# Attention with one factor product, one mask and a two-part Y; weights decoded 768 columns at a time; a new order for the first 512 tokens

## The chip, the cores and the metric

The kernel runs on one core of one Trainium2 chip. The metric is the device time of one execution in microseconds (us), the median of three runs. On the core work TensorE (matrix products; PE in the views, PEld its weight loads), VectorE (DVE), ScalarE (ACT), GpSimd (POOL) and SyncE (SP), which here only issues DMA transfers. Each engine runs its instructions in the order in which they are written and waits for semaphores where it needs another's result.

## The reference

A linear attention with a decaying state, then two expert layers in a row, all of them on float32 inputs (the weights are float64, as they come out of a product with a float64 scalar):

```python
for t in range(S):                      # S = 768, 4 batches, 8 heads, D = 48
    cur = np.einsum('bhd,bhe->bhde', u[None] * kt, vt)
    y[:, :, t] = np.einsum('bhd,bhde->bhe', rt, state + cur)
    state = wt[:, :, :, None] * state + np.einsum('bhd,bhe->bhde', kt, vt)
...
h = x @ w_in                            # x: 3072 x 384, w_in: 384 x 2048
x = (h * np.clip(h + 3.0, 0.0, 6.0) / 6.0) @ w_out
...
a, b = x @ w_a, x @ w_b                 # 384 x 1536 each
out = a * b @ w_out2
```

## The kernel before

**Units.** The tokens are cut into 6 blocks of 128 per batch; a block of a batch is a unit, 24 in all, unit n being block n // 4 of batch n % 4. The attention of a unit works on two chunks of 64 tokens. Its factors lie with the head dimension on partitions: 48 rows of even heads from partition 0, 48 of odd heads from 64, and 4 head pairs side by side along the columns. One tile `rkw` of 1545 columns holds r (0 to 511), k (512 to 1023) and the decays w (from 1024).

**One unit, by its letters** (the order below is written in them; a number after a letter is the unit, slot or weight piece). R, N, V load r/k/w, the token-major copy (r, k, v) and v. z (L191) and s (L215) scan the decays backwards and forwards; c (L199, L200) takes the chunk products pc and their reciprocals as seeds of s. k (L206) multiplies k by z, a and b (L223) multiply r by pp for the even and the odd heads: a on VectorE, b on GpSimd, both into the tile `yo`. T transposes k on TensorE, t copies the result. A (L298, L299) is k against r within a chunk, on TensorE; m and M (L303) mask its two halves into `yo`. So `yo` holds, per head half, the scaled r (48 rows) and under or over it the masked A (64 rows), with zero rows between. K is k against v, in PSUM; u and f (L337) scale the state by pc for the two chunks, v and g (L344, L345) copy it beside the loaded v in the tile `vs`, and e and h (L355) add K to it. Y (L366) is then one product of 128 or 112 rows per head and chunk: scaled r with the state and masked A with v in one. d, D, o form r·u·k per head (for units 0 and 1 by TensorE, `PE_DOT`; for the others by GpSimd products and a reduction on VectorE, L259), O (L266) multiplies it by v, x (L380) adds it to Y. X transposes the result, H and L (L395, L400) split it into a high part and a rest, `xh` and `xl`.

**Expert layers.** They work in slots: 128 columns of the first layer's 2048 on 512 tokens. P (L497, nine products into one bank) is the first layer, r y G l its activation and its split (L518, L522, L526, L531), Q (L550, nine products) the second. A slot needs `xh` and `xl` of all four units of a block. 96 slots for both layers are followed by 72 steps of the third and fourth.

**Weights.** They come as float64 and are decoded by integer steps in half pieces of 384 columns, 32 for the first two layers and 36 later: W loads one into `raw` (3 buffers), i (L451, L452) scales its two words on ScalarE, j (L457) shifts and J (L461) sets the sign on VectorE, w (L467) adds on GpSimd, p (L482) takes the high part on ScalarE and n (L487) the low part on VectorE or GpSimd.

**Order.** `prepare` (L719) loads unit 0, sets constants and zeros in `vs`, and gives TensorE idle products. `start` (L864) then goes through the string `CFG["start"]`, letter by letter: units 0 to 7, slots 0 to 15 and half pieces 0 to 31. `CFG["pool"]` lists what goes to GpSimd there instead of VectorE. From slot 16 on `run` (L808) goes slot by slot: elementwise work of the attention stages that are due, P, then T and A of a unit in its stage 1, the activation, Q of the slot before, weight work, and the other stages' products. A unit passes stages 0 to 5 in six slots, a new unit starts every third slot, and units 8 to 23 go that way. SP issues loads in the same order: R for the unit after next in stage 1, V in stage 3, N in stage 4.

Of the kernel before, what the change touches and what calls it, by code (L numbers as in the profile page):

```python
# [964 lines left out]
```

## Time and profile before

| what | us |
|---|---|
| median of 3 runs | 1040.18 (1039.97 to 1040.42) |
| span of the profiled execution | 1038.7 |
| TensorE busy in the span | 989.7 (95%) |
| VectorE busy | 656.7 (63%) |
| ScalarE busy | 376.3 (36%) |
| GpSimd busy | 245.3 (24%) |

The profile is of one execution. It gives that execution's span from the first to the last instruction; a run's time also holds what lies around the span, and the median stands 1.5 us above this span. Shares are means over the whole span, which has a hand-ordered part and a regular one, so they are read together with the stretches and the chain of waits.

### The profile page before, as it was taken

Reading aid. Unit: us, or ns where it says so; the run is one execution under the profiler, and the core shown is the slowest. Engines: PE = TensorE matmul, PEld = TensorE weight load, DVE = VectorE, ACT = ScalarE, POOL = GpSimd, SP = SyncE. Lnnn points to the kernel's source line nnn. Section 1 sums busy time; section 2 is a strip of 40 time slices with the busy share of each in tenths; the row PEclk is TensorE's granted clock in tenths of the full one; section 3 lists DMA queues with packets and bytes.
Section 4 is the critical chain, followed back from the end, with each engine's and each line's share of the span. In section 5 each row is a group of like instructions: output and inputs, shape, how many; then the busy total and the mean of one; then the engine's idle time right before and its main releaser. Section 6 shows DMA issues by size and latency. Waiting matters only on the chain.

```text
span 1038.7 us, 15835 instructions
## 1 busy us (share of the span) xinstructions
PE 989.7 (95%) x6339; PEld 813.4 (78%) x6342; DVE 656.7 (63%) x1012; ACT 376.3 (36%) x727; POOL 245.3 (24%) x221
## 2 busy tenths in 40 slices
PE   7687889999999999999999999999999999999996
PEld 4465668778777877777777888888888888888886
DVE  8999996875775776776688886444444444422222
ACT  3356553233323333333667643222222222222121
POOL 5777772321230321132244531000000000000000
PEclk8698889999999999999999999999999999999999
DMA  9254463231222232120243531111111110100001
GB/s 323 94 175 152 138 205 123 70 116 56 99 70 84 72 114 91 62 70 1 92 132 123 180 119 32 51 42 31 51 42 32 58 53 22 41 21 13 19 1 34
DMA packets 33299, 85.79 MB, mean 83 GB/s; under 512 B 4160, under 2 KB 10816, under 8 KB 33216
## 3 DMA queue, kind: packets, MB, share of 16 engines
q1 hardware_dynamic: 33216, 84.69, 24.4%
q8 instruction: 52, 0.85, 0.3%
q14 instruction: 31, 0.25, 0.1%
HBM read 75.23 MB, written 9.44 MB: 82 GB/s over the span
## 4 chain that ended last, share of the span: by engine, by line
PE 65%; DVE 24%; issue 5%; ACT 4%; POOL 1%; DMA 0%; DVEq 0%; POOLq 0%
PE ab L497 29%; PE oa L618 15%; PE x2a L550 10%; PE h L497 9%; DVE t L522 3%; DVE wa L457 3%; DVE z L191 2%; ACT gh L526 2%; DVE gl L531 2%; DVE pp L215 2%; DVE yo L303 2%; DVE w L487 2%; DVE st L355 1%; DVE wa L461 1%; DVE sp L337 1%
## 5 line engine op out<-in xcount | busy, mean ns | idle before, releaser
L497 PE MATMUL ab<-xh_b,w 128*128 128x512 f32 x864 | 225.1, 396 | 0.0
L497 PEld LDWEIGHTS ab<-xh_b,w 128*128 128x128 f32 x864 | 161.2, 188 | 33.3 <-DVE t L522 0.4
L497 PE MATMUL h<-xh_a,w 128*128 128x512 f32 x576 | 164.8, 421 | 16.0 <-DVE w L487 9.3
L596 DVE TENSOR_TENSOR ta<-ab,ta 128x512 f32<-128x512 f32 x72 | 49.8, 691 | 198.3 <-PE ab L497 198.3
L550 PE MATMUL x2a<-gh,w 128*128 128x512 f32 x576 | 152.6, 400 | 1.4 <-ACT gh L526 1.2
L497 PEld LDWEIGHTS h<-xh_a,w 128*128 128x128 f32 x576 | 107.9, 196 | 43.1 <-DVE w L487 10.9
L550 PEld LDWEIGHTS x2a<-gh,w 128*128 128x128 f32 x576 | 106.1, 188 | 28.6 <-ACT gh L526 2.5
L497 PE MATMUL ab<-xl_b,w 128*128 128x512 f32 x432 | 124.1, 395 | 0.0
L531 DVE TENSOR_TENSOR gl<-t,gh 128x512 fp32r<-128x512 f32 x91 | 82.0, 901 | 60.3 <-ACT gh L526 55.0
L618 PE MATMUL oa<-w,ph 128*128 128x384 f32 x576 | 113.4, 338 | 0.0
L618 PEld LDWEIGHTS oa<-w,ph 128*128 128x128 f32 x576 | 102.9, 188 | 6.5 <-DVE x2e L562 0.2
L526 ACT CAST gh<-t 128x512 fp32r<-128x512 f32 x96 | 59.5, 620 | 130.2 <-DVE t L522 126.9
L599 ACT CAST ph<-ta 128x512 fp32r<-128x512 f32 x72 | 44.7, 621 | 165.9 <-DVE ta L596 165.9
L595 ACT COPY ta<-ab 128x512 f32<-128x512 f32 x72 | 42.2, 586 | 166.6 <-PE ab L497 166.6
L467 POOL TENSOR_TENSOR wa<-wa,raw 128x384 int32<-128x384 int32 x68 | 75.8, 1115 | 106.2 <-DVE wa L461 74.0
L522 DVE SCALAR_TENSOR_TENSOR t<-t,h 128x512 f32<-128x512 f32 x96 | 65.3, 681 | 52.4 <-ACT t L518 51.8
L497 PEld LDWEIGHTS ab<-xl_b,w 128*128 128x128 f32 x432 | 81.2, 188 | 19.8
L497 PE MATMUL h<-xl_a,w 128*128 128x512 f32 x288 | 85.4, 406 | 0.0
L518 ACT ACTIVATE t<-h,half 128x512 f32<-128x512 f32 x96 | 66.0, 687 | 46.8 <-PE h L497 43.5
L550 PE MATMUL x2a<-gl,w 128*128 128x512 f32 x288 | 82.9, 396 | 0.0
L600 DVE TENSOR_TENSOR pl<-ta,ph 128x512 fp32r<-128x512 f32 x72 | 49.9, 693 | 49.4 <-ACT ph L599 49.4
L223 POOL TENSOR_TENSOR yo<-rkw,pp 48x512 f32<-48x512 f32 (+1 forms) x25 | 37.3, 1493 | 160.1 <-DVE pp L215 83.8
(89 smaller groups left out, 1264.6 us busy)
## 6 DMA issues: line engine op xcount, KB each, us to landing
raw<-in_wall_dram SPq DMA_DIRECT2D x68, 384.0 KB, 3.1
rkw<-in_rkw_dram SPq DMA_DIRECT2D x23, 772.5 KB, 5.1
nat<-in_nat_dram SPq DMA_DIRECT2D x22, 576.0 KB, 3.9
cw<-in_rkw_dram SPq DMA_DIRECT2D x24, 260.5 KB, 2.7
vs<-in_vst_dram SPq DMA_DIRECT2D x48, 96.0 KB, 2.7
x2d<-x2e SPq DMA_DIRECT2D x18, 256.0 KB, 2.5
x2r<-x2d SPq DMA_DIRECT2D x18, 256.0 KB, 2.9
out_dram<-oe SPq DMA_DIRECT2D x24, 192.0 KB, 2.0
```

The source lines that it names most:

```text
L467: nc.gpsimd.tensor_tensor(out=a, in0=a, in1=raw[n][:, :, 0], op=ALU.add)
L497: nc.tensor.matmul(out=o, lhsT=lt, rhs=rt, start=(i == 0), stop=(i == 3 * n - 1))
L518: nc.scalar.activation(out=t, in_=hb[s], func=ACTF.Relu, bias=half, scale=1.0 / 6.0)
L522: nc.vector.scalar_tensor_tensor(out=t, in0=t, scalar=1.0, in1=hb.pop(s), op0=ALU.min, op1=ALU.mult)
L526: nc.scalar.copy(out=gh, in_=G["t", s])
L531: ve(f"l{s}").tensor_tensor(out=gl, in0=G.pop(("t", s)), in1=G[s][0].bitcast(F32), op=ALU.subtract)
L550: nc.tensor.matmul(out=acc1[i][k], lhsT=w[:, e, 384 + k * 128:512 + k * 128], rhs=rt, start=(f == 0 and e == 0 and rt is gh), stop=(f == N ...
L595: nc.scalar.copy(out=t, in_=a)
L596: nc.vector.tensor_tensor(out=t, in0=bb, in1=t, op=ALU.mult)
L599: nc.scalar.copy(out=gh, in_=t)
L600: nc.vector.tensor_tensor(out=gl, in0=t, in1=gh.bitcast(F32), op=ALU.subtract)
L618: nc.tensor.matmul(out=acc2[j][b][:, 0:384], lhsT=lt[:, b * 128:(b + 1) * 128], rhs=rt, start=(f == 0 and rt is wh and lt is ph), stop=(la ...
```

## The change

Five things are changed.

**One factor product.** The two scans now write into one tile `zp` of 1042 columns, the forward products in front and the backward ones behind, laid out so that r and k, which lie side by side in `rkw`, are multiplied by it in one instruction of 1024 columns on VectorE (k). a and b are gone. A reads both its operands from `rkw`.

**One mask.** A's halves come out in the order of the partitions, so m masks all 128 rows in one instruction, into a tile `am` of its own. M, `yo`, the zeroing of `vs` and the copies of the state into `vs` (v, g) are gone.

**Y from two products.** Per head and chunk, one product of the scaled r (48 rows) with the scaled state `sp` and one of the masked A (64 rows) with v, added in PSUM; even and odd heads go to two banks, and x adds them in two instructions. For units 0 to 3 the first chunk has no state and needs the second product alone. T and A of a unit now stand at the end of the slot with the other stages' products.

**Weights.** A piece has 768 columns and `raw` and `wa` two buffers each; J writes into `raw`, w is two additions on GpSimd or, for the seven pieces named in `CFG["fast"]`, one instruction of 1536 half words on VectorE, and n is always on VectorE.

**The order.** All units up to 7 form the dot by TensorE (`N_DOT = 8`), `CFG["pool"]` is empty, and the string is new. `prepare`, as before, begins with `load_rkw(0)`.

```diff
-    "fast": 'b6',
+    "pool": "",
+    "fast": "w4 w5 w6 w9 w11 w14 w15",
-        "z0 R1 c0 s0 a0 d0 D0 o0 b0 k0 z1 c1 A0 s1 W0 M0 i0 j0 W1 J0 m0 N0 d1 k1 i1 j1 a1 J1 R2 b1 O0 T0 t0 "
+        "R0 W0 V2 V1 V0 V3 R1 d0 N0 z0 D0 o0 c0 s0 W1 i0 k0 j0 A0 J0 T0 m0 w0 t0 z1 R2 N1 K0 c1 p0 d1 O0 s1 D1 e0 "
...
+    def a_s(n):
+        u = U[n]
+        nc.vector.tensor_tensor_scan(
+            out=u["zp"][:, 0:519], data0=u["rkw"][:, 1024:1543], data1=seed[:, 0:519], initial=0.0,
+            op0=ALU.mult, op1=ALU.add,
+        )
+
     def a_k(n):
         u = U[n]
+        rk = u["rkw"][:, 0:1024].rearrange("p (q i) -> p q i", i=64)
+        f = u["zp"][:, 0:1040].rearrange("p (q i) -> p q i", i=QL)[:, :, 0:64]
+        ve(f"k{n}").tensor_tensor(out=rk, in0=rk, in1=f, op=ALU.mult)
...
-                nc.tensor.matmul(out=a[64:128, sl], lhsT=kk[0:48, sl], rhs=Y[0:48, 0, sl], start=True, stop=True)
-                nc.tensor.matmul(out=a[0:64, sl], lhsT=kk[64:112, sl], rhs=Y[64:112, 1, sl], start=True, stop=True)
+                for e in (0, 64):
+                    nc.tensor.matmul(
+                        out=a[e:e + 64, sl], lhsT=kk[e:e + 48, sl], rhs=rr[e:e + 48, sl], start=True, stop=True,
+                    )
+    def a_m(n):
         u = U[n]
         nc.vector.tensor_tensor(
+            out=u["am"].rearrange("p (q i) -> p q i", i=64), in0=u["ap"].rearrange("p (q i) -> p q i", i=64),
+            in1=mask.rearrange("p (o i) -> p o i", o=1).to_broadcast([128, 8, 64]), op=ALU.mult,
         )
...
     def a_Y(n):
+        yp = u["yp"] = [att_bank(f"Y{e}", n) for e in range(2)]
         for p in range(NP):
+            for i in range(2):
                 for c in range(2):
                     sl = slice(p * 128 + c * 64, p * 128 + c * 64 + 64)
+                    first = j == 0 and c == 0
+                    if first and i == 0:
+                        continue
+                    for e in range(2):
+                        lo = 64 * e
+                        if i == 0:
+                            lt, rt = u["rkw"][lo:lo + 48, sl], u["sp", c][lo:lo + 48, p]
+                        else:
+                            lt, rt = u["am"][lo:lo + 64, sl], u["vs"][lo:lo + 64, p, c]
+                        nc.tensor.matmul(
+                            out=yp[e][64 * c:64 * c + 64, p * D:p * D + D], lhsT=lt, rhs=rt,
+                            start=i == 0 or first, stop=i == 1,
+                        )
...
+    def w_sign(i):
+        t = raw[i]
         nc.vector.scalar_tensor_tensor(
+            out=t[:, :, 0], in0=t[:, :, 1], scalar=-2 ** 31, in1=t[:, :, 0], op0=ALU.bitwise_and, op1=ALU.bitwise_or,
         )
+    def w_add(i, eng):
+        a, t = raw.pop(("a", i)), raw[i]
+        cuts = (0, 768) if eng is nc.vector else (0, 384, 768)
+        for c0, c1 in zip(cuts, cuts[1:]):
+            eng.tensor_tensor(out=a[:, c0:c1], in0=a[:, c0:c1], in1=t[:, c0:c1, 0], op=ALU.add)
...
-            for n, sg in act:
-                if sg == 1:
-                    att_pe(n, sg)
...
             for n, sg in act:
-                if sg != 1:
-                    att_pe(n, sg)
+                att_pe(n, sg)
```

What moves is shown at three places. The first is the beginning of SP's queue of loads (`rkw0` is unit 0's r, k and w, `raw` a weight piece, `vs` and `avs` hold v, `nat` the token-major copy). Before:

```order
L147 DMA rkw0_102<-in_rkw_dram 128x521
L148 DMA rkw0_102<-in_rkw_dram 128x1024
L727 DMA cst_sb_79<-in_cst_dram 128x194
L728 DMA u_pair_81<-in_ud_dram 128x8
L150 DMA rkw1_137<-in_rkw_dram 128x1545
L442 DMA raw0_179<-in_wall_dram 128x768
L442 DMA raw1_186<-in_wall_dram 128x768
```

Now:

```order
L136 DMA rkw0_99<-in_rkw_dram 128x521
L137 DMA rkw0_99<-in_rkw_dram 128x1024
L685 DMA cst_sb_79<-in_cst_dram 128x194
L686 DMA u_pair_81<-in_ud_dram 128x8
L136 DMA rkw0_124<-in_rkw_dram 128x521
L137 DMA rkw0_124<-in_rkw_dram 128x1024
L401 DMA raw0_127<-in_wall_dram 128x1536
L155 DMA avs2_95<-in_vst_dram 128x384
L155 DMA vs1_90<-in_vst_dram 128x384
L155 DMA vs0_89<-in_vst_dram 128x384
L155 DMA avs3_96<-in_vst_dram 128x384
L139 DMA rkw1_133<-in_rkw_dram 128x1545
```

Unit 0's two loads stand there twice, into two buffers, a weight piece of twice the width follows, and unit 1's load stands behind four loads of v.

The second is the end of the hand-written order on VectorE, before slot 16 (`w15` is the low part of the last weights, `gl` the rest of an activation, `xl_a1` the rest of a unit's output, `t` an activation). Before:

```order
L380 TENSOR_TENSOR nat7_1358<-Y_7_1557,nat7_1358 128x384
L522 SCALAR_TENSOR_TENSOR t13_1600<-t13_1600,h13_1539 128x512
L522 SCALAR_TENSOR_TENSOR t14_1603<-t14_1603,h14_1585 128x512
L400 TENSOR_TENSOR xl_a1_1137<-X_7_1596,xh_a1_1136 128x3x128
L457 TENSOR_SCALAR wa31_1620<-raw31_1487 128x384
L461 SCALAR_TENSOR_TENSOR wa31_1620<-raw31_1487,wa31_1620 128x384
L531 TENSOR_TENSOR gl12_1639<-t12_1524,gh12_1637 128x512
L531 TENSOR_TENSOR gl13_1652<-t13_1600,gh13_1650 128x512
L531 TENSOR_TENSOR gl14_1669<-t14_1603,gh14_1667 128x512
L522 SCALAR_TENSOR_TENSOR t15_1654<-t15_1654,h15_1608 128x512
L355 TENSOR_TENSOR st3_94<-K1_7_1498,sp7_1_1522 112x192
L531 TENSOR_TENSOR gl15_1697<-t15_1654,gh15_1695 128x512
```

Now:

```order
L360 TENSOR_TENSOR xl_a1_903<-X_6_1460,xh_a1_902 128x3x128
L446 TENSOR_TENSOR w15_1489<-wa15_1421,w15_1489 128x768
L309 TENSOR_TENSOR st3_94<-K0_7_1495,sp7_0_1423 112x192
L490 TENSOR_TENSOR gl14_1524<-t14_1468,gh14_1492 128x512
L298 TENSOR_TENSOR sp7_1_1526<-st3_94,pc7_1313 112x192
L309 TENSOR_TENSOR st3_94<-K1_7_1496,sp7_1_1526 112x192
L360 TENSOR_TENSOR xl_a1_903<-X_5_1253,xh_a1_902 128x3x128
L481 SCALAR_TENSOR_TENSOR t15_1567<-t15_1567,h15_1514 128x512
L337 TENSOR_TENSOR nat7_1181<-Y0_7_1530,nat7_1181 128x4x48
L337 TENSOR_TENSOR nat7_1181<-Y1_7_1531,nat7_1181 128x4x48
L490 TENSOR_TENSOR gl15_1583<-t15_1567,gh15_1581 128x512
L360 TENSOR_TENSOR xl_a1_903<-X_7_1585,xh_a1_902 128x3x128
```

Before, unit 7's `xl_a1` stood ahead of the last half piece's decoding and of slot 15's activation; now it is the last, behind `w15`, slot 15's activation and unit 7's two additions.

The third is TensorE's stream in slot 20 of the regular part (`X_8` transposes unit 8's output, `T_9` and `A_9` are unit 9's first products, `h21` and `x2a` expert work). Before:

```order
L298 MATMUL A_9_1945<-yo1_88,rkw9_1656 64x64
L299 MATMUL A_9_1945<-yo1_88,rkw9_1656 64x64
L550 MATMUL x2a1_0_1795<-gh19_1893,w3_744 128x512 x2
L550 MATMUL x2a1_1_1796<-gh19_1893,w3_744 128x512 x2
L550 MATMUL x2a1_2_1797<-gh19_1893,w3_744 128x512 x2
L550 MATMUL x2a1_0_1795<-gl19_1895,w3_744 128x512
L550 MATMUL x2a1_1_1796<-gl19_1895,w3_744 128x512
L550 MATMUL x2a1_2_1797<-gl19_1895,w3_744 128x512
L387 MATMUL X_8_1978<-cst_sb_79,nat8_1483 128x128 x3
L497 MATMUL h21_1997<-xh_a1_1136,w5_845 128x512 x6
L497 MATMUL h21_1997<-xl_a1_1137,w5_845 128x512 x3
```

Now:

```order
L509 MATMUL x2a1_0_1660<-gh19_1772,w3_427 128x512 x2
L509 MATMUL x2a1_1_1661<-gh19_1772,w3_427 128x512 x2
L509 MATMUL x2a1_2_1662<-gh19_1772,w3_427 128x512 x2
L509 MATMUL x2a1_0_1660<-gl19_1774,w3_427 128x512
L509 MATMUL x2a1_1_1661<-gl19_1774,w3_427 128x512
L509 MATMUL x2a1_2_1662<-gl19_1774,w3_427 128x512
L347 MATMUL X_8_1850<-cst_sb_79,nat8_1257 128x128 x3
L244 MATMUL T_9_1854<-cst_sb_79,rkw9_1564 128x112 x4
L265 MATMUL A_9_1859<-rkw9_1564 64x64 x16
L456 MATMUL h21_1890<-xh_a1_902,w5_698 128x512 x6
```

A of unit 9 stood in front of slot 19's second-layer products and X of unit 8 behind them; now X, T and A follow one another behind these products.

## Rows read from the trace of the kernel before

**Rows 1.** The page, parts 1 and 2: engines' totals; VectorE in 40 slices, busy tenths.

```profile
PE 989.7 (95%) x6339; PEld 813.4 (78%) x6342; DVE 656.7 (63%) x1012; ACT 376.3 (36%) x727; POOL 245.3 (24%) x221
DVE  8999996875775776776688886444444444422222
```

**Rows 2.** By stretch: its length, busy PE, PEld, DVE, ACT, POOL; PEclk, DMA, GB/s.

```profile
25.00:150.00 125.00, 94.43 (x869) 72.71 (x870) 123.50 (x172) 68.33 (x149) 92.77 (x77) 0.84 0.44 145
0.00:163.70 163.70, 126.62 (x1140) 95.95 (x1144) 153.80 (x215) 82.22 (x177) 113.59 (x103) 0.85 0.54 182
165.00:578.00 413.00, 408.98 (x3041) 323.06 (x3041) 299.97 (x486) 176.33 (x338) 109.49 (x97) 1.00 0.25 85
```

**Rows 3.** The chain of waits in order of time: start us, us, what.

```profile
154.50 10.49 PE x2a L550 x45
164.99 2.11 PE h L497 x9
167.09 2.10 PE x2a L550 x9
172.75 0.01 PE A L299
```

**Rows 4.** Groups of instructions, whole run: busy us, mean ns | idle before, releaser.

```profile
L457 DVE TENSOR_SCALAR wa<-raw 128x384 int32<-128x384 int32 x68 | 38.9, 574 | 0.0
L461 DVE SCALAR_TENSOR_TENSOR wa<-raw,wa 128x384 int32<-128x384 int32 x68 | 58.6, 861 | 1.9
L487 DVE TENSOR_TENSOR w<-wa,w 128x384 fp32r<-128x384 f32 x36 | 30.0, 838 | 1.0
L531 DVE TENSOR_TENSOR gl<-t,gh 128x512 fp32r<-128x512 f32 x91 | 82.0, 901 | 60.3 <-ACT gh L526 55.0 <-PE x2a L550 5.3
```

**Rows 5.** Single lines on VectorE, whole run: count, shortest/middle/longest ns, first and last start.

```profile
L457 DVE TENSOR_SCALAR wa<-raw x68: 329/355/1655, 14.7 to 627.0; 128x384 int32<-128x384 int32 x68
L461 DVE SCALAR_TENSOR_TENSOR wa<-raw,wa x68: 506/560/1740, 15.8 to 627.3; 128x384 int32<-128x384 int32 x68
L487 DVE TENSOR_TENSOR w<-wa,w x36: 544/652/1622, 53.5 to 633.9; 128x384 fp32r<-128x384 f32 x36
L531 DVE TENSOR_TENSOR gl<-t,gh x91: 679/693/1512, 60.7 to 576.7; 128x512 fp32r<-128x512 f32 x91
L206 DVE TENSOR_TENSOR rkw<-rkw,z x19: 639/641/1778, 8.9 to 473.0; 128x512 f32<-128x512 f32 x19
L223 DVE TENSOR_TENSOR yo<-rkw,pp x23: 655/683/1664, 6.6 to 474.9; 64x512 f32<-64x512 f32 x22, 48x512 f32<-48x512 f32 x1
L303 DVE TENSOR_TENSOR yo<-A,cst_sb x48: 654/689/698, 14.1 to 484.1; 64x512 f32<-64x512 f32 x48
L380 DVE TENSOR_TENSOR nat<-Y,nat x23: 526/545/553, 33.6 to 491.7; 128x384 f32<-128x384 f32 x23
```

**Rows 6.** The same view, GpSimd's additions of the weight decoding.

```profile
L467 POOL TENSOR_TENSOR wa<-wa,raw x68: 1006/1030/1957, 17.0 to 628.7; 128x384 int32<-128x384 int32 x68
```

**Rows 7.** Timeline of VectorE from 0 to 4 us, first and last row.

```profile
0.88 0.27 DVE L721 MEMSET wz<- 128x256 uint32 x1 [0.88 <-PEq L952]
...
3.56 1.24 DVE L191 TENSOR_TENSOR_SCAN z<-rkw,ones_rev 128x520 f32<-128x520 f32 x1 [1.17 <-DMA rkw<-in_rkw_dram]
```

**Rows 8.** Timeline of SP's DMA queue: the load of unit 1 is issued.

```profile
2.62 0.43 SPq L150 DMA_DIRECT2D rkw<-in_rkw_dram  x1
```

**Rows 9.** DMA issues: count, KB each, middle us from issue to landing.

```profile
raw<-in_wall_dram SPq DMA_DIRECT2D x68, 384.0 KB, 3.1
rkw<-in_rkw_dram SPq DMA_DIRECT2D x23, 772.5 KB, 5.1
```

**Rows 10.** TensorE's waits from 165 to 580 us: total us, times, longest.

```profile
PE A L299 <- POOL yo L223: 2.1, 5, 0.4
```

**Rows 11.** Timeline of TensorE: one unit's K, one unit's Y.

```profile
16.14 0.68 PE L326 MATMUL K<-nat,kt 64*64 64x48 f32 x32
...
321.20 1.14 PE L366 MATMUL Y<-vs,yo 128*64 128x48 f32 x32
```

More of the change, by code (lines that the diff above doesn't have):

```diff
@@ L95, in rwkv_moe_kernel @@
     seed = cp.tile([128, 8 * QL], F32, name="seed")
-    yo = [cp.tile([128, 2, 512], F32, name=f"yo{i}") for i in range(2)]
-    vs = [cp.tile([128, 2, NP, 2, D], F32, name=f"vs{i}") for i in range(2)]
+    am = [cp.tile([128, 512], F32, name=f"am{i}") for i in range(2)]
+    vs = [cp.tile([128, NP, 2, D], F32, name=f"vs{i}") for i in range(2)]
     st = [cp.tile([128, NP, D], F32, name=f"st{b}") for b in range(B)]
@@ L114, in att_bank @@
             i = min(ok, key=lambda i: last.get(i, -1))
-            users = "q" if kind == "Y" and f"x{n}" in POOL else USERS[kind]
-            held[i] = {f"{u}{n}" for u in users}
+            held[i] = {f"{u}{n}" for u in USERS[kind]}
         else:
@@ L129, in rwkv_moe_kernel @@
     units = [(j, b) for j in range(NBLK) for b in range(B)]
-    U = [{"yo": yo[n % 2], "vs": vs[n % 2]} for n in range(len(units))]
+    U = [{"am": am[n % 2], "vs": vs[n % 2]} for n in range(len(units))]
     FIRST = (2, 3)
@@ L188, in a_z @@
         w = u["rkw"][:, 1024:1545]
-        z = ap_.tile([128, 521], F32, name=f"z{n}", tag="z", bufs=1)
-        u["z"] = z
+        if 0 < n <= max(FIRST):
+            zp = spare([128, 1042], f"zp{n}")
+        else:
+            zp = ap_.tile([128, 1042], F32, name=f"zp{n}", tag="zp", bufs=1)
+        u["zp"] = zp
         nc.vector.tensor_tensor_scan(
-            out=z[:, 520:0:-1], data0=w[:, 520:0:-1], data1=ones_rev, initial=0.0, op0=ALU.mult, op1=ALU.add,
+            out=zp[:, 1038:518:-1], data0=w[:, 520:0:-1], data1=ones_rev, initial=0.0, op0=ALU.mult, op1=ALU.add,
         )
@@ L324, in a_K @@
                 lo, hd = 64 * e, 2 * DM + (2 * p + e) * 48
-                m = 64 if n < WIDE_KV and e == 0 else 48
+                m = 64 if e == 0 else 48
                 nc.tensor.matmul(
@@ L339, in state_scale @@
         )
-    def state_put(n, c):
-        u = U[n]
-        V, sp = u["vs"], u["sp", c]
-        nc.scalar.copy(out=V[0:48, 0, :, c, :], in_=sp[0:48])
-        nc.scalar.copy(out=V[64:112, 1, :, c, :], in_=sp[64:112])
     def state_add(n, c):
@@ L461, in w_sign @@
+    def w_sign(i):
+        t = raw[i]
         nc.vector.scalar_tensor_tensor(
-            out=a, in0=raw[n][:, :, 1], scalar=-2 ** 31, in1=a, op0=ALU.bitwise_and, op1=ALU.bitwise_or,
+            out=t[:, :, 0], in0=t[:, :, 1], scalar=-2 ** 31, in1=t[:, :, 0], op0=ALU.bitwise_and, op1=ALU.bitwise_or,
         )
-    def w_add(n):
-        a = raw.pop(("a", n))
-        nc.gpsimd.tensor_tensor(out=a, in0=a, in1=raw[n][:, :, 0], op=ALU.add)
-        raw[n] = a.bitcast(F32)
-    def w_dec(n):
-        if wide:
-            for fn in (w_scale, w_shift, w_sign, w_add):
-                fn(n)
@@ L475, in w_high @@
-    def w_high(n):
-        i, q = divmod(n, 2)
-        if q == 0:
-            if i in (28, 29):
-                W[i] = ap_.tile([128, 2, 768], F32R, name=f"w{i}", tag="rkw")
-            else:
-                W[i] = wp.tile([128, 2, 768], F32R, name=f"w{i}", tag="w", bufs=16)
-        nc.scalar.copy(out=W[i][:, 0, q * 384:(q + 1) * 384], in_=raw[n])
-    def w_low(n, eng):
-        i, q = divmod(n, 2)
-        hi, lo = (W[i][:, e, q * 384:(q + 1) * 384] for e in range(2))
-        eng.tensor_tensor(out=lo, in0=raw.pop(n), in1=hi.bitcast(F32), op=ALU.subtract)
@@ L489, in w_split, with w_dec @@
-    def w_split(n, eng):
-        w_high(n)
-        w_low(n, eng)
+    def w_add(i, eng):
[3 more added lines that the diff above has]
+            eng.tensor_tensor(out=a[:, c0:c1], in0=a[:, c0:c1], in1=t[:, c0:c1, 0], op=ALU.add)
+        raw[i] = a.bitcast(F32)
+    def w_dec(i):
+        if wide:
+            w_scale(i)
+            w_shift(i)
+            w_sign(i)
+            w_add(i, nc.gpsimd)
@@ L493, in mm3, with w_high, w_low, w_split @@
+    def w_high(i):
+        if i in (28, 29):
+            W[i] = ap_.tile([128, 2, 768], F32R, name=f"w{i}", tag="rkw")
+        else:
+            W[i] = wp.tile([128, 2, 768], F32R, name=f"w{i}", tag="w", bufs=16)
+        nc.scalar.copy(out=W[i][:, 0], in_=raw[i])
+    def w_low(i, eng):
+        eng.tensor_tensor(out=W[i][:, 1], in0=raw.pop(i), in1=W[i][:, 0].bitcast(F32), op=ALU.subtract)
+    def w_split(i):
+        w_high(i)
+        w_low(i, nc.vector)
     def mm3(o, parts):
@@ L664, in rwkv_moe_kernel, with w_step @@
     pend = []
-    def w_step(s, k):
-        for n in pend[:k]:
-            w_split(n, nc.gpsimd if n % 2 == 0 else nc.vector)
-        del pend[:k]
+    def w_step():
+        for i in pend:
+            w_split(i)
+        pend.clear()
     def w_step2(s):
@@ L868, in start @@
                 continue
-            if tok == "P0":
+            if tok == "P1":
+                ring["free"].remove(4)
+            elif tok == "Q0":
                 ring["free"] = [5, 6, 7]
@@ L877, in rwkv_moe_kernel @@
         start()
-        wnext[0] = 2 * NF1
-        for _ in range(3):
+        wnext[0] = NF1
+        for _ in range(2):
             w_ahead()
@@ L887, in rwkv_moe_kernel @@
             wnext[0] = 0
-            for _ in range(3):
+            for _ in range(2):
                 w_ahead()
```

156 lines of the change are left out of this document (47 added, 109 removed), and 30 rows, old and new, of the table CFG.

## The prediction

> **What bounds the kernel now.** I read the page first, then busy times by stretch, then the chain of waits, then the groups and single lines of the engines that wait. On the page [rows 1] TensorE is busy 95% of the span, but VectorE's slices say where it isn't: VectorE stands at 9 tenths or nearly so in the first six slices and falls after that. The stretches [rows 2] make it plain. From 25 to 150 us VectorE works 123.50 of 125 us and TensorE 94.43; from 165 to 578 us TensorE works 408.98 of 413. So there are two stages with two limits: the hand-ordered head (the first 512 tokens), limited by VectorE, and everything after it, limited by TensorE. The border is seen in the chain [rows 3]: five second-layer groups are run off in one piece from 154.50, and at 164.99 slot 16 starts, the first product on tokens 512 to 1023. From there on the work is fixed. A change gains what it brings slot 16 forward, and what it takes from TensorE's own stream behind it.
>
> VectorE's head is long for a second reason. The four forms in [rows 4] have means of 574, 861, 838 and 901 ns over the run, while the same lines have low or middle values of 355, 560, 544 and 693 ns [rows 5]. Both inputs, or the only one, lie in SBUF there, and the long cases stand where GpSimd works. The excess is 68 x 0.219 + 68 x 0.301 + 36 x 0.294 + 91 x 0.208 = 64.9 us against 245.3 us of GpSimd work [rows 1], 0.26 us per us; other forms add some, so I take 0.3. Lines that read PSUM (L303, L380) hardly spread [rows 5].
>
> **What the change takes from VectorE in the head.** Eight units and 16 weight pieces. Gone: one of two masks, 8 x 0.69 = 5.5; k and a apart, 3 x 0.64 + 7 x 0.68 = 6.7; six dot reductions of 384 columns at L380's 0.545, 3.3; the shift and sign of 32 half pieces, 32 x (0.355 + 0.560) = 29.3; 18 low halves, 18 x 0.544 = 9.8. Together 54.6 us, all by [rows 5].
>
> **What it adds there.** Longer operands: between 384 and 512 columns L487 and L206 differ by 97 ns, L487 and L531 by 149, so 0.76 to 1.16 ns a column; I take 0.96, and for all wide forms together the two ends make 5 us either way. The joint factor on 1024 columns: 0.641 + 512 x 0.96 = 1.13, x 8 = 9.0. Seven more r x k products for the dot, 0.64 each: 4.5. Y's add in two pieces, plus one that was on GpSimd: 8 x 0.2 + 0.5 = 2.1. Shift and sign at 768: shift between 0.355 (nothing for the columns) and 0.71 (two halves), 0.53 in the middle; sign 0.560 + 0.37 = 0.93; 16 x 1.46 = 23.4. Low parts at 768, all on VectorE: 16 x 0.91 = 14.6. Seven integer additions come from GpSimd to VectorE as an instruction on 1536 half words, which the trace doesn't show: 0.91 if it goes by 768 words, 0.560 + 1152 x 0.96 = 1.67 if by its 1536 elements. I take 1.67, since every row here goes by elements: 11.7. Five gl from GpSimd, 3.5; four scalings of 192 columns, about 0.36, 1.4. Together 70.2, so VectorE's own work grows by 15.6 us.
>
> **What the stretching gives back.** GpSimd keeps nine pieces' additions (18 instructions) and eight products with the dot. At 1.03 us [rows 6] that is 26.8 us in place of 113.6 [rows 2]. 86.8 us less at 0.3: 26.0 us. VectorE's busy time up to its last head instruction goes from 153.8 [rows 2] to 153.8 + 15.6 - 26.0 = 143.4.
>
> **The start gets later.** VectorE waits 0.88 + 1.17 = 2.05 us today and starts its first scan at 3.56 [rows 7]. In the new order the setup loads unit 0 and the order opens with R0, which loads it again, into another buffer, and that copy is the one read. It stands in the queue where unit 1's equally large load stands now: issued at 2.62 [rows 8], 5.1 us to landing [rows 9], so 7.7. VectorE's new first instruction needs r and k of it: 4.1 us lost. The wide weight piece behind it is needed only after some 5 us of work on unit 0, so I cost it at nothing; if it lands late, unit 1's scan is late next.
>
> **Where the head ends.** Now unit 7 is finished before the last weight pieces, and slot 16 waits only for TensorE's backlog. In the new order unit 7's last step L7 is VectorE's last instruction, and slot 16 needs it. Behind the last low part of the weights come about 4.9 us of VectorE work, but TensorE's path is longer: slot 15's products 2.1 [rows 3], Y of unit 7 1.1 [rows 11], a second-layer group 2.1, and about 1.3 for transposes, copy and subtraction: 6.6. VectorE's other idle time is the unknown. Between 25 and 150 us it is now 1.5 us [rows 2]. In the new order n-to-product-to-y, sign-to-add-to-low and the two raw buffers (add, load, scale) leave about a microsecond beyond their latencies at some 15 places, counting VectorE's work between the two ends of each chain. And TensorE must put 15 first- and 14 second-layer groups of 2.1 and four units' attention at about 5, some 81 us, into about 90 us of VectorE's work (143.4 less four units at about 7 and six pieces at about 3.5 that come before). Low end 1.5; high end 15, half of the 30.6 us that TensorE idles there now [rows 2]. I take 5, near the low end, since VectorE alone is the longest queue. Slot 16 then starts at 2.05 + 4.1 + 143.4 - 4.9 + 5 + 6.6 = 156.3, **8.7 us earlier**.
>
> **Behind the head.** TensorE waited 2.1 us in five places for GpSimd's half of r x pp [rows 10]; GpSimd has no part in it any more: -2.1. T and A move to the slot's end, behind X of the unit before in 12 of 16 units; a first group after attention work takes 2.30 in place of 2.10 [rows 3], so 12 x 0.2 = -2.4. K's first halves become 64 wide in 16 units: +0.8. r now stays in use up to Y, so SP's load of the unit after next waits two slots longer, with the v load behind it; the next scan comes three slots later, a load takes 5.1 [rows 9], so nothing. The late weights come in two whole buffers instead of three halves; two pieces follow within two slots (8.4 us), where addition, load and scaling want about 10: ScalarE waits perhaps 1 us that reaches TensorE: +1.
>
> Y is the open price: 64 instructions instead of 32 per unit. 32 of Y take 1.14 us, 36 ns each; 32 of K, which also go to all four quarters of the array and to a bank per row half, take 0.68, 21 ns each [rows 11]. At K's pace 64 take 1.36, at Y's 2.28. I take K's, less half for the overhead at its ends, +0.1 a unit, +1.6 in 16 units. The Trainium skill ("TensorE: Matmul & The Clock Gate", "Wait — 56ns, not 53.3ns?") says that start-to-start never drops below about 25 ns however few the columns; by that, as an estimate, Y would take 1.6 us and the sum would be 5.8 us higher. This case's trace doesn't agree for work spread over the quarters: K's 21 ns include its ends.
>
> Sum: -2.1 - 2.4 + 0.8 + 1 + 1.6 = -1.1, with the head **-9.8 us**. The profiled execution spans 1038.7 us; the median of the runs, 1040.18, is 1.5 above it for what lies around the span, which stays. **1040.2 - 9.8 = 1030.4 us.**
>
> **Rivals.** (a) VectorE starves: the order leaves no slack, one engine waits for the other, and idle time is 14 instead of 5. For it: TensorE would be 90% full in the same stretch. Against: 1.5 us today. 1030.4 + 9 = 1039.4. (b) On the other side: the new Y's instructions start one behind the other at Y's present pace, in each unit behind the head, where TensorE has no slack. 16 x 1.14 = 18.2 in place of 1.6: 1047. It decides from 0.7 us a unit on. For it: Y's own row; against: K's. (c) Something per instruction holds Y's starts back halfway between the two paces, at 28.5 ns: 64 take 1.82, 0.68 more a unit, 16 x 0.68 = 10.9 in place of 1.6: 1039.7. For it: Y has more columns to load per instruction than K; against: that should cost a tenth, not a third. The skill's rule above is of this kind. (d) The change doesn't free VectorE, as the stretching isn't GpSimd's doing: 26 us stay, 1056. Against it: the spread is on SBUF forms alone. (e) Better: the additions take 0.91 and idle stays at 1.5: -5.3 - 3.5, 1021.6.
>
> **How the numbers follow.** Forecast 0.52, (a) 0.14, (b) 0.11, (c) 0.08, (d) 0.05, (e) 0.10. A measurement of this kernel tells 0.2%, 2.1 us, from nothing. Faster: the forecast and (e) whole, 0.62, and the lower parts of (a) and (c), 0.09: 0.71. Within 0.2%: the middle of (a) and of (c), 0.11. Slower: (b), (d) and the tops of (a) and (c), 0.18. The range from 1019 to 1045 leaves out (d), most of (b) and the bottom of (e), under 0.2; the wide forms' and the idle time's ends lie inside.
>
> **What would show it.** First VectorE work on unit 0 at about 7.7. VectorE busy about 143 us up to L7, GpSimd about 27. Sign at 768 columns near 0.93, the integer addition near 1.67. Slot 16 at 156. Y's 64 in 1.2 to 1.4 us. No wait of A for GpSimd. It is wrong if VectorE idles over 14 us before slot 16, if Y takes 0.7 us more a unit than now, or if SBUF forms stay stretched with GpSimd idle.

## The result and the profile after

The changed kernel takes 1026.71 us (median of 4 runs, 1025.84 to 1030.04) where the kernel before takes 1040.30 beside it (1039.97 to 1041.06): ratio 0.9874, 95% interval 0.9858 to 0.9889. The forecast was 1030.4, range 1019 to 1045. The profiled execution spans 1024.1 us.

The page's totals of engines and VectorE's and the clock's slices, after (against [rows 1]):

```profile
PE 985.8 (96%) x7079; PEld 816.2 (80%) x7079; DVE 590.2 (58%) x914; ACT 337.8 (33%) x542; POOL 117.4 (11%) x114
DVE  7879887656755765674677776444444444322222
PEclk6589999999999999999999999999999999999999
```

Busy time by stretch, after (columns as in [rows 2]; 152.43 is the end of L7, VectorE's last instruction of the head):

```profile
0.00:152.43 152.43, 125.14 (x1374) 101.61 (x1375) 127.60 (x197) 68.93 (x110) 37.63 (x32) 0.82 0.50 174
8.00:52.00 44.00, 26.10 (x388) 23.96 (x389) 39.17 (x57) 14.73 (x25) 15.25 (x12) 0.50 0.65 240
60.00:152.43 92.43, 88.81 (x845) 71.56 (x846) 80.45 (x125) 48.87 (x75) 21.34 (x15) 0.95 0.43 146
165.00:578.00 413.00, 409.23 (x3532) 323.19 (x3531) 266.59 (x420) 156.87 (x245) 69.14 (x72) 1.00 0.26 88
```

VectorE works 127.6 us to the head's end where it worked 153.8, and GpSimd 37.6 where it worked 113.6. But VectorE is no longer full: from 60 us on it is busy 80.45 of 92.43 us, and TensorE 88.81.

TensorE's timeline, after: a group that waits in the head, and slot 16's first group:

```profile
97.95 0.50 PE L456 MATMUL h<-xh_a,w 128*128 128x512 f32 x1
100.37 2.37 PE L456 MATMUL h<-xh_a,w 128*128 128x512 f32 x5 [1.92 <-DVE w L446]
...
151.89 1.67 PE L456 MATMUL h<-xh_a,w 128*128 128x512 f32 x6 [0.57 <-ACT xh_a L355]
```

Slot 16 starts at 151.89 instead of 164.99 [rows 3], 13.1 us earlier. From there to the end it takes 1024.1 - 151.9 = 872.2 us, before 1038.7 - 165.0 = 873.7. So 13.1 of the span's 14.6 us are won ahead of slot 16. The chain of waits behind the head, after: a unit's Y in 1.08 us, and X, T, A and the next first-layer group in one block:

```profile
171.93 1.08 PE Y L328 x64
...
177.39 0.33 PE X L347 x3
177.72 0.38 PE T L244 x4
178.10 1.08 PE A L265 x32
179.18 2.30 PE h L456 x9
```

Groups on VectorE and GpSimd from 0 to 150 us, after (busy us, mean ns | idle before, releaser; to be held against [rows 4 to 6]):

```profile
L420 DVE SCALAR_TENSOR_TENSOR raw<-raw 128x768 int32<-128x768 int32 x16 | 15.9, 991 | 0.4 <-ACT raw L411 0.3
L446 DVE TENSOR_TENSOR w<-wa,w 128x768 fp32r<-128x768 f32 x16 | 15.3, 959 | 0.4 <-ACT w L443 0.3
L416 DVE TENSOR_SCALAR wa<-raw 128x768 int32<-128x768 int32 x16 | 9.6, 601 | 0.0
L428 DVE CUSTOM_DVE_ANT_0 wa<-raw,wa 128x1536 uint16<-128x1536 uint16 x7 | 6.7, 955 | 0.1
...
L428 POOL TENSOR_TENSOR wa<-wa,raw 128x384 int32<-128x384 int32 x18 | 27.2, 1532 | 64.3 <-DVE raw L420 27.2 <-DVE wa L416 19.1 <-issue 17.9
```

Sign (0.991) and low part (0.959) stand near their predicted 0.93 and 0.91; the integer addition on VectorE takes 0.955, not 1.67: as long as the subtraction of 768 words, though it has 1536 elements.

### The profile page after: what moved, and what is told of

Its sections match the earlier page's. It is cut to its first block, busy times and chain, and to the rows that moved or that the text cites. A ratio compares the mean times of both kernels' runs of the same rounds, so it can differ in the third digit from the quotient of the medians.

```text
span 1024.1 us, 16627 instructions
## 1 busy us (share of the span) xinstructions
PE 985.8 (96%) x7079; PEld 816.2 (80%) x7079; DVE 590.2 (58%) x914; ACT 337.8 (33%) x542; POOL 117.4 (11%) x114
## 4 chain that ended last, share of the span: by engine, by line
PE 79%; DVE 5%; issue 5%; POOL 2%; ACT 2%; DMA 1%; SPq 0%; POOLq 0%; ACTq 0%
PE ab L456 29%; PE h L456 15%; PE oa L577 15%; PE x2a L509 14%; POOL wa L428 2%; PE Y L328 2%; PE A L265 2%; PE K L287 1%; DVE raw L420 1%; PE T L244 1%; DVE gl L490 1%; DVE zp L190 1%; ACT raw L411 1%; PE X L347 1%; ACT raw L410 1%
## 5 line engine op out<-in xcount | busy, mean ns | idle before, releaser
L456 PE MATMUL h<-xh_a,w 128*128 128x512 f32 x576 | 158.9, 411 | 2.6 <-DVE w L446 1.9
L456 PEld LDWEIGHTS h<-xh_a,w 128*128 128x128 f32 x576 | 104.6, 190 | 27.3 <-DVE w L446 2.8
L490 DVE TENSOR_TENSOR gl<-t,gh 128x512 fp32r<-128x512 f32 x96 | 74.0, 772 | 55.1 <-ACT gh L485 50.3
L558 ACT CAST ph<-ta 128x512 fp32r<-128x512 f32 x72 | 44.7, 621 | 163.8 <-DVE ta L555 163.8
L428 POOL TENSOR_TENSOR wa<-wa,raw 128x384 int32<-128x384 int32 x54 | 63.8, 1203 | 176.0 <-DVE raw L420 138.9
L456 PEld LDWEIGHTS h<-xl_a,w 128*128 128x128 f32 x288 | 55.0, 191 | 13.4
```

The lines of the kernel that those rows point to most:

```text
L428: eng.tensor_tensor(out=a[:, c0:c1], in0=a[:, c0:c1], in1=t[:, c0:c1, 0], op=ALU.add)
L456: nc.tensor.matmul(out=o, lhsT=lt, rhs=rt, start=(i == 0), stop=(i == 3 * n - 1))
L490: ve(f"l{s}").tensor_tensor(out=gl, in0=G.pop(("t", s)), in1=G[s][0].bitcast(F32), op=ALU.subtract)
L558: nc.scalar.copy(out=gh, in_=t)
```

## The experiments

Every kernel is the changed one with one edit. "Slot 16" and "rest" are of the profiled execution: when slot 16 starts, and how long it is from there to the span's end.

| kernel | median us (runs) | ratio to before | slot 16 | rest |
|---|---|---|---|---|
| before | 1040.3 (4) | 1 | 165.0 | 873.7 |
| changed | 1026.71 (4) | 0.9874 (0.9858 to 0.9889) | 151.9 | 872.2 |
| e1 one load | 1023.79 (4) | 0.9836 (0.9816 to 0.9857) | 148.1 | 873.6 |
| e2 idle products | 1029.46 (4) | 0.9896 (0.988 to 0.9913) | 153.9 | 873.3 |
| e4 GpSimd reads | 1059.51 (1) | | 184.3 | 873.4 |
| e5 GpSimd writes | 1030.25 (1) | | 156.0 | 872.5 |
| e6 Y in quarters | 1028.05 (2) | 0.988 (0.986 to 0.99) | 151.8 | 874.2 |
| e7 half pieces | 1023.26 (4) | 0.9825 (0.9809 to 0.9842) | 153.7 | 869.3 |
| e8 additions on GpSimd | 1032.53 (4) | 0.9922 (0.9905 to 0.9938) | 156.8 | 873.7 |
| e9 T and A in the slot | 1026.96 (4) | 0.9877 (0.9845 to 0.991) | 151.4 | 872.7 |
| e11 early work | 1028.4 (2) | 0.9886 (0.9868 to 0.9904) | 154.9 | 872.1 |
| e12 late work | 1031.76 (2) | 0.9918 (0.99 to 0.9936) | 157.7 | 873.1 |
| e13 late halves, one load | 1020.98 (5) | 0.9813 (0.98 to 0.9827) | 149.2 | 869.4 |
| e14 idle before P8 | 1028.31 (2) | 0.9885 (0.9867 to 0.9903) | 153.3 | 873.6 |

Where a tail is not edited, the rest lies between 872.1 and 873.7. Most of this spread, and part of what before and changed differ by, stands behind TensorE's last product. TensorE's timelines, that product in before, changed, e7 and e13:

```profile
1030.45 0.34 PE L618 MATMUL oa<-w,pl 128*128 128x384 f32 x1
1016.67 0.33 PE L577 MATMUL oa<-w,pl 128*128 128x384 f32 x1
1014.43 0.34 PE L583 MATMUL oa<-w,pl 128*128 128x384 f32 x1
1010.73 0.34 PE L586 MATMUL oa<-w,pl 128*128 128x384 f32 x1
```

From slot 16 to the end of that product it takes 865.8 us before and 865.1 to 865.4 in the changed kernel and all whose tail is not edited, but 866.9 in e6, 864.5 in e9, 861.1 in e7 and 861.9 in e13. What follows it takes 7.0 to 8.5 us, whatever the edit. The start of slot 16 is less steady: work ahead of an edit came up to 3.4 us later than in the changed kernel (last section), and each kernel has one profile.

### e1: unit 0 loaded once

```diff
-        "R0 W0 V2 V1 V0 V3 R1 d0 ...
+        "W0 V2 V1 V0 V3 R1 d0 ...
```

> The order without its R0, so that unit 0 is loaded once, by the setup. Theory 1: the head is a chain from the first load over units 0 to 3 to the first slot, and from there TensorE is full (88.8 of 92.4 us between 60 and 152.4 us), so an earlier start goes through to the end. Unit 0's r and k then land where they did before, at about 5.0 instead of 7.6 us; slot 16 starts 2.5 to 3.5 us earlier, the time is that of the changed kernel less 3. Rival: VectorE's later waits absorb the earlier start (it idles 25 us in the head); slot 16 moves by less than 1 us.

VectorE's timeline, its first work on unit 0, after and then in e1:

```profile
7.59 0.69 DVE L205 TENSOR_TENSOR nat<-rkw 112x512 f32<-112x512 f32 x1 [5.21 <-DMA rkw<-in_rkw_dram]
```

```profile
4.87 0.69 DVE L205 TENSOR_TENSOR nat<-rkw 112x512 f32<-112x512 f32 x1 [2.49 <-DMA rkw<-in_rkw_dram]
```

The second load costs 2.72 us at the start, 3.8 at slot 16 and 2.9 in the median; these differ by no more than the head does without an edit. The new order has to wait even for the first load until 4.87, because it begins with r x k; the old one began with the decays at 3.56 [rows 7].

### e4, e5 and e8: what GpSimd does to VectorE

"Stretch" means here that an instruction takes longer than the same one elsewhere. e4 puts 96 additions and e5 96 memsets of an idle tile on GpSimd, between tokens of the head. Neither changes what is computed.

```diff
+            if tok[0] in "zskmjnyl":
+                nc.gpsimd.tensor_tensor(out=dum[:, 0:260], in0=ones_rev[:, 0:260], in1=ones_rev[:, 260:520], op=ALU.add)
```

```diff
+            if tok[0] in "zskmjnyl":
+                nc.gpsimd.memset(dum, 1.0)
```

> The changed kernel with 96 additions of 260 columns on GpSimd strewn over the head, that read two constants and write a tile nobody reads: some 75 us more GpSimd work, about as much as the change took away. Theory 1 (GpSimd's reads of SBUF stretch VectorE): the durations of VectorE's head instructions grow by 0.3 to 0.4 us per us, 22 to 30 us in sum, and slot 16 starts 8 to 20 us later, at 160 to 172. Rival (the stretching had another cause, such as the number of VectorE's instructions or the DMA traffic): durations grow by less than 5 us, slot 16 moves by less than 3.

> The same 96 places, with a memset of 640 columns in each: as much GpSimd time, but no reads of SBUF. If reads are what stretches VectorE: durations grow by less than 5 us and slot 16 stays within 3 us of 151.9. If any GpSimd work does it: as with the additions, 160 to 172.

Groups from 0 to 150 us in e4, then in e5:

```profile
L447 DVE TENSOR_TENSOR w<-wa,w 128x768 fp32r<-128x768 f32 x13 | 16.6, 1282 | 6.3 <-ACT w L444 6.3
L421 DVE SCALAR_TENSOR_TENSOR raw<-raw 128x768 int32<-128x768 int32 x14 | 16.5, 1188 | 0.0
L417 DVE TENSOR_SCALAR wa<-raw 128x768 int32<-128x768 int32 x13 | 11.0, 843 | 0.0
```

```profile
L826 POOL MEMSET dum<- 128x640 f32 x96 | 62.7, 653 | 4.8 <-POOLq L906 0.3
...
L447 DVE TENSOR_TENSOR w<-wa,w 128x768 fp32r<-128x768 f32 x16 | 15.9, 999 | 3.5 <-ACT w L444 3.4
L421 DVE SCALAR_TENSOR_TENSOR raw<-raw 128x768 int32<-128x768 int32 x16 | 15.3, 962 | 0.3 <-ACT raw L412 0.3
```

In e4 VectorE's work up to slot 16 grows from 127.6 to 155.7 us while GpSimd's grows from 37.6 to 149.6: 0.25 us per us. That is a little under the 0.3 to 0.4 expected, but on 112 us more of GpSimd's work, not 75, and slot 16 comes 32.4 us later, far outside the 8 to 20. In e5 GpSimd has 61 us more and VectorE 1.3, and the low part and the sign stay as they were. So the stretch is real and comes from GpSimd's reads, not from its being busy. The Trainium skill ("SBUF — State Buffer", "Who interferes with whom") says the same: a VectorE instruction with two inputs in SBUF contends with a GpSimd instruction that reads SBUF, not with one that only writes. Here 1.282 and 0.999 us of the same subtraction agree. The shift, which has one input, is stretched in e4 as well: 0.843 us as against 0.601 in the changed kernel. e5's 4.1 us at slot 16, over the 3 allowed, are not stretch. Its low parts wait 3.4 us for ScalarE's high copies, 0.3 in the changed kernel, since the weight additions in front of these stand behind memsets in GpSimd's queue; that this is all of it is not shown.

e8 gives the seven additions back to GpSimd:

```diff
-    "fast": "w4 w5 w6 w9 w11 w14 w15",
+    "fast": "",
```

> The seven integer additions on VectorE (0.955 us each, 6.7 in sum) go to GpSimd, two of 384 columns each. Theory: GpSimd works 14 to 21 us more in the head, which stretches VectorE by 3 to 8 us (0.22 to 0.41 us per us), so little is won or lost: slot 16 within 2 us of 151.9, time 1024 to 1029. Rival 1: the stretch doesn't matter and VectorE gains 6.7: slot 16 4 to 6 us earlier, 1021. Rival 2: the longer chain sign, two additions, high, low holds up the products: slot 16 over 3 us later, 1030 or more.

GpSimd works 18.9 us more (56.5), VectorE 127.3 against 127.6: the 6.7 us taken away come back as stretch, 0.34 per us of GpSimd. That is the theory's half; the other half is rival 2: the chain through two additions is longer, and slot 16 comes 4.9 us later. VectorE idles 5.3 us more up to slot 16, and 2.8 of that are low parts that wait for the high copy behind the additions. VectorE's waits up to 150 us, after and then in e8:

```profile
DVE w L446 <- ACT w L443: 0.3, 1, 0.3
DVE w L446 <- ACT w L443: 3.1, 4, 1.0
```

### e6: the order of Y's instructions

```diff
-            for i in range(2):
+            for e in range(2):
                 for c in range(2):
...
-                    for e in range(2):
+                    for i in range(2):
```

> Y's 64 instructions in another sequence: the two products of one output piece, which use the same quarter of the array, follow each other directly. Theory: Y costs 1.08 us for 64 because neighbouring instructions go to four different quarters; now two in a row share one, so Y takes 1.6 to 2.3 us and the 16 units behind the head cost 8 to 20 us more (1035 to 1047). Rival: only the number of instructions counts, 17 ns each wherever they go: Y stays at 1.08 us and the time at 1026.7.

In the chain of e6 the same unit's Y takes 1.18 us (the chain runs over 61 of the 64), where it took 1.08:

```profile
171.80 1.18 PE Y L328 x61
```

That is 0.10 us more a unit, 18 ns an instruction instead of 17, and 1.6 in 16 units, which agrees with the 866.9 us up to TensorE's last product; the median of 1028.05 is inside the changed kernel's own spread. So the order costs something, but a fifth or less of what the theory wanted. The rival nearly holds: it isn't the alternation of quarters that makes Y quick. Per instruction Y's old form took 36 ns [rows 11], with up to 64 more rows each.

### e11, e12, e2 and e14: which engine sets the head's pace

```diff
+            if tok in "s0 k0 m0 s1 f0 k1 s2 k2".split():                # e11
+            if tok in "n12 j13 y11 l11 j14 n13 j15 n14".split():        # e12
+                nc.vector.memset(dum, 0.0)
```

> Eight idle memsets on VectorE (128 x 520, 0.49 us each, 3.9 in sum) stand in its queue in the first 45 us of the head. Theory: VectorE sets the pace there, so all of it shows: slot 16 starts 3.3 to 4.2 us later than 151.9. Rival: TensorE's work alone sets the head's end: under 1 us.

> The same eight memsets, but in VectorE's queue between 115 and 145 us. Theory: there TensorE sets the pace (busy 8.00 of 8 us in most windows), VectorE has gaps, and slot 16 starts at most 1.5 us later than 151.9. Rival, the prediction's own view that VectorE is the longest queue up to the head's end: 3.3 to 4.2 us later, as with the early ones.

In e11 slot 16 comes 3.0 us later, a little under what was expected. Compared instruction by instruction with the changed kernel, VectorE is 0.3 us late at its first load and 3.3 behind the last memset at 36 us, so 3.0 of the 3.9 us go through there. e12 refutes the theory in its sharp form: slot 16 comes 5.8 us later. But VectorE is already 3.4 us late ahead of the first memset (a first load that lands 0.8 later, and the clock, last section), and 5.8 behind the last: 2.4 of the 3.9 us go through, more than the theory's 1.5 and less than the rival's 3.3. Both queues are nearly full behind 60 us and feed each other, and most of what is put into VectorE's is seen.

e2 gives TensorE 45 idle products in six places up to 40 us, of the kind the order before had; e14 gives it eight ahead of the ninth first-layer group (for that the zero tile `wz` gets memory of its own).

```diff
-... z0 D0 o0 c0 ... A0 J0 T0 m0 ... R2 N1 K0 c1 ... K1 z2 X0 h0 ... J2 J3 T2 N4 t2 j3 K2 z4
+... z0 D0 E5 o0 c0 ... A0 J0 T0 E2 m0 ... R2 N1 K0 E4 c1 ... K1 z2 X0 E12 h0 ... J2 J3 T2 E2 N4 t2 j3 K2 E20 z4   # e2
-... i10 l5 P8 w9 ...
+... i10 l5 E8 P8 w9 ...   # e14
```

> The changed order with idle products on TensorE (45 in six places before the first slot), as the order before had them. Theory 1: TensorE's granted clock is 0.50 from 8 to 52 us in the changed kernel because the new order has none, and the half clock lengthens the products that VectorE waits for (3.0 us for Y of unit 2 at 51 us, 0.9 and 0.7 for A). With them the clock stands near 1.00 by 30 us, VectorE's waits before 60 us shrink by 3 to 5 us, and slot 16 starts 2 to 4 us earlier. Rival: the idle products stand in front of real ones, or the waits are replaced by others; slot 16 within 1 us or later.

> Eight idle products (1.7 us at full clock) stand ahead of the ninth first-layer group, which waits 1.9 us at 98.5 us for VectorE's low part and runs its next five products in 2.37 us where they take 1.43 at the full clock. Theory: with the engine busy through the wait the granted clock stays at 1.00 and these products and the three behind them run 1.4 to 1.6 us shorter, so the stretch behind comes 1 to 1.6 us earlier: slot 16 at 150.3 to 150.9. Rival: the work behind waits for VectorE anyway or the idle products are themselves in the way: slot 16 within 0.5 us of 151.9 or later.

In e2 the granted clock is 0.85 up to 25 us and 0.79 from 25 to 60, and still nothing is won: median and slot 16 come 2.7 and 2.0 us later, about the scatter. TensorE's timeline shows why. The products of Y that VectorE waits longest for, those of unit 2 at 48.64 us, follow those of unit 1, and these stand behind a wait of TensorE for VectorE. All of them run at the lower clock again, 0.50 from 44.7 to 54.9 us:

```profile
44.97 0.35 PE L328 MATMUL Y<-sp,rkw 48*64 48x48 f32 x2 [5.03 <-DVE sp L298]
```

VectorE then waits 2.92 us for them, as against 3.01 in the changed kernel. In e14 TensorE's timeline and VectorE's show two things:

```profile
99.24 1.90 PE L385 MATMUL heatx<-wz 128*128 128x512 bf16 x7
101.29 1.78 PE L456 MATMUL h<-xh_a,w 128*128 128x512 f32 x6 [0.15 <-PE heatx L385]
102.91 0.86 PE L456 MATMUL h<-xl_a,w 128*128 128x512 f32 x3
...
117.03 0.69 DVE L205 TENSOR_TENSOR nat<-rkw 112x512 f32<-112x512 f32 x1 [2.64 <-DMA rkw<-in_rkw_dram]
```

The products run at the full clock, and VectorE's place in its queue goes from 1.5 us late to 0.1 late. But e9, which has no idle products there, waits 1.92 us as the changed kernel does and still runs these five products at the full clock, and VectorE gains 1.2 us there too. TensorE's timeline in e9:

```profile
100.24 1.43 PE L456 MATMUL h<-xh_a,w 128*128 128x512 f32 x5 [1.92 <-DVE w L446]
```

So the grant at this place differs without an edit, and that the idle products raised it is not shown. Twelve microseconds on, VectorE waits 2.64 us for unit 7's load instead of 1.18, and is 1.2 late again. That load is issued behind Y of unit 5, since Y now reads r from the buffer that it fills. But it is issued no later than in the changed kernel; it lands later, 7.1 us after its issue instead of 5.6. SP's queue and VectorE's start on the load, after, and SP's queue in e14:

```profile
110.18 1.89 SPq L139 DMA_DIRECT2D rkw<-in_rkw_dram  x1
115.84 0.69 DVE L205 TENSOR_TENSOR nat<-rkw 112x512 f32<-112x512 f32 x1 [1.18 <-DMA rkw<-in_rkw_dram]
```

```profile
109.91 0.42 SPq L139 DMA_DIRECT2D rkw<-in_rkw_dram  x1
```

In e1, e6, e9 and e13 it takes 4.6 to 6.6 us. So slot 16 at 153.3 says nothing against the theory, and the clock nothing for it: e14 leaves open what idle products are worth here.

### e7, e9 and e13: the wide decode and the merged block

e7 cuts every 768-column decode instruction into two (and the scalings, the shift and both splits alike):

```diff
-        cuts = (0, 768) if eng is nc.vector else (0, 384, 768)
+        cuts = (0, 384, 768)
...
-        nc.scalar.copy(out=W[i][:, 0], in_=raw[i])
+        for q in (slice(0, 384), slice(384, 768)):
+            nc.scalar.copy(out=W[i][:, 0, q], in_=raw[i][:, q])
```

> Every decode instruction on 768 columns (shift, sign, addition on VectorE, both scalings, high copy, low part) becomes two on 384. VectorE then works about 8.4 us more in the head, 5.3 of it on the ten pieces decoded before 105 us. Theory: VectorE sets the pace up to about 100 us and TensorE behind that, so the first product of slot 16 comes 3 to 5.5 us later than in the changed kernel (151.9) and the time is 1030 to 1032. Rival 1: VectorE sets the whole head: 8.4 us later, 1035. Rival 2: the width brings nothing, the new order alone made the gain: under 1.5 us later.

VectorE works 130.2 us up to slot 16 where the changed kernel works 127.1: 3.1 more, not 8.4. Slot 16 comes 1.8 us later, less than the theory wanted and no more than it moves without an edit, so what the width is worth at the head's end stays open. But the time is 3.4 us **shorter**: none of the three said so. The rest is 869.3 instead of 872 to 874. Waits of ScalarE from 500 to 575 us, after and then in e7 (us, times, longest):

```profile
ACT w L443 <- POOL wa L428: 9.4, 11, 0.9
```

```profile
ACT w L447 <- POOL wa L431: 2.7, 11, 0.3
```

There a late piece falls into nearly every slot. ScalarE's high copy of a whole piece waits for both GpSimd additions, and the next activation's split stands behind it; TensorE waits for that from 165 to 580 us, after:

```profile
PE x2a L509 <- ACT gh L485: 1.4, 2, 0.9
PE oa L577 <- DVE x2e L521: 0.5, 1, 0.5
```

In e7 neither row is there. The same wait is seen in more places in front of the weight loads of the second layer, after, in e7 and in e13 (engine PEld, 165 to 580 us):

```profile
PEld x2a L509 <- ACT gh L485: 3.6, 6, 1.3
PEld x2a L515 <- ACT gh L491: 0.4, 1, 0.4
PEld x2a L518 <- ACT gh L494: 1.4, 2, 0.7
```

e9 puts T and A back in front of Q:

```diff
                 L3_pe(sb)
+            for n, sg in act:
+                if sg == 1:
+                    att_pe(n, sg)
```

> Behind the head the transposes and A of a unit go back to their old place, between the slot's first products and its second-layer group. Theory: the merged block with X saves the 0.2 us that a first group after attention work takes longer, 12 times: 2.4 us slower than the changed kernel, 1029. Rival: merging them moves nothing, within 1 us of 1026.7. The head is unchanged: slot 16 at 151.9.

The rival holds: the median is the changed kernel's, and up to TensorE's last product e9 takes 0.6 us less, not 2.4 more. e13 joins what helped, halves for the 18 late pieces alone (`i >= NF1`) and e1's edit:

> Decode in halves for the 18 weight pieces behind the head only (the 16 of the head stay at 768 columns), and unit 0 loaded once. Theory: the whole-piece decode costs TensorE 3 to 4 us at slots 67 to 80, where ScalarE stands behind GpSimd's addition, so from slot 16 to the end it takes 869 to 870 us instead of 872 to 874; the one load brings slot 16 to 148 to 149. Span about 1018, time 1019 to 1021, faster than both kernels. Rival: what half pieces won came from the head's other order of work or from noise, then 873 remain behind slot 16 and the time is 1023 to 1024.

1020.98 us, ratio 0.9813 (0.98 to 0.9827), faster than both kernels, with the two parts where they were expected: slot 16 at 149.2, rest 869.4.

## Why the prediction was right, and where not

**Start.** 7.7 forecast, 7.59 measured. The loss of 4.1 us is right; only 2.7 of it are the second load's (e1).

**VectorE's work.** 143.4 us forecast, 127.6 measured. Two terms were mis-sized. The seven integer additions take 0.955 us, not 1.67: 5.0 us less; rival (e)'s price was near. The rest, about 11 us, is stretch. An estimate from the traces takes each form's shortest duration in its run as unstretched: by that, the head's instructions on VectorE are stretched by 50.3 us in all before and by 11.4 after, so 38.9 came back where 26.0 were forecast; the other work grew by some 2 us more than forecast. GpSimd's work fell by less than forecast, 76.0 us and not 86.8, mostly since its 18 additions take 1.532 us each and not 1.03. So the price of 0.3 was too low: in the head of before it is 50.3 / 113.6 = 0.44. The prediction took it from means over the whole run, and the shift, whose mean there is 574 ns [rows 4], has 822 in the head (before, 0 to 163.7 us):

```profile
L457 DVE TENSOR_SCALAR wa<-raw 128x384 int32<-128x384 int32 x32 | 26.2, 822 | 0.0
```

0.25 in e4 and 0.34 in e8 show that there is no one price; it depends on which instructions meet. Rival (d) is out by e4 and e5.

**Idle time.** This step failed. VectorE was to idle 5 us beyond start and end. It idles 24.8 us up to L7, 6.1 of them at the start and 1.7 at the end by the prediction's own sum, so some 17 where 5 were forecast. That is more than rival (a)'s 14, and over the 14 that the prediction named as a sign that it is wrong. The biggest single one is 3.0 us at 51 us, for Y of unit 2, at the end of a stretch from 8 to 52 us in which TensorE, busy 26.1 of 44 us, is granted the clock 0.50, its level of 1.2 GHz. Idle products don't cure that (e2), and how much of the wait is the clock's is not shown. "VectorE alone is the longest queue" is wrong from 60 us on, where TensorE is 96% full and VectorE 87% (e12). Some 16 us less work and 12 more idle time nearly cancelled, which is luck: slot 16 came at 151.9, 4.4 us ahead of the forecast 156.3. Nor does slot 16 start behind L7: its first product waits for ScalarE's `xh_a` of unit 7 and starts 0.5 us before L7 ends.

**Behind the head.** -1.1 forecast, -1.5 measured, by other terms; only 0.7 of it lies ahead of TensorE's last product. The wait for GpSimd (2.1) is gone as said. Y costs nothing more: 1.08 us a unit, so 17.3 us in 16 units where the old form took 17.1 (group start to group start); rivals (b) and (c) are out. The Trainium skill ("TensorE: Matmul & The Clock Gate", "Wait — 56ns, not 53.3ns?") puts the least time from start to start at about 25 ns; these instructions, which use a quarter of the array each, start every 17 ns on average, so here the measurement disagrees. The merged block brings nothing (e9). The 2.30 us for which the prediction names [rows 3] don't stand there but in this row of the chain of before, and a first group behind A takes 2.30 after the change too, in the block above.

```profile
172.75 2.30 PE x2a L550 x9
```

Beyond the wait A became 0.14 us quicker a unit (2.2 in 16) and K 0.07 (1.1), where K was to cost 0.8; X takes 1.0 more. Without the late weights that makes -2.1 + 0.2 - 2.2 - 1.1 + 1.0 = -4.2, and 865.8 - 4.2 = 861.6 us up to TensorE's last product stands between e7's 861.1 and e13's 861.9. The late weights give back 3 to 4 us of it where the prediction had 1: this term was mis-sized, since it counted ScalarE's wait for the buffers and not the activation that stands behind the wait for GpSimd's second addition in ScalarE's queue.

So the direction and the mechanism, GpSimd's reads, were right. That the total was within 4 us is in part luck: the head's two errors had opposite signs, and so had the terms behind it.

## What to carry to other kernels

Take work from GpSimd that reads SBUF, not work that only writes, when VectorE's inputs lie in SBUF, and count what comes back as stretch before moving additions there. Price the stretch in the stage that the change touches, not over the run. Wider instructions save overhead (3.1 us of VectorE's work in e7) and can lose more: at the end of an in-order queue that waits for another engine, two halves finish sooner than one whole (e13). When one engine is relieved, name the queue that is next and add the waits between the two. And where the part ahead of an edit moves by itself, as here by up to 3.4 us, compare profiles instruction by instruction from the edit on.
